# One decode layer on one core: a shorter VectorE program, other load sizes, result stores on exchanged queues, and buffers on lines of 512 bytes

## Chip, cores, metric

One core of a Trainium2 chip. The time is that of the device for one execution, in microseconds (us). The profile's span is shorter than that time: it runs from the first to the last record of the engines, and here that difference (1.24 to 1.55 us on average) turns out to matter. The granted TensorE clock was full (1.00) in most stretches and half (0.50) in some, 0.896 on average in the profile of before.

## The reference, cut to what matters

A decode step for one token: attention over a window of 4096 keys and values, beside a feed-forward block. Everything is bf16.

```python
xn = _layernorm(x)                                # x is [1, 1, 1024]
q  = xn @ wq                                      # wq [1024, 4096], 32 heads of 128
p  = softmax(q @ k[-4096:].T * 128**-0.5)         # 4 groups of keys, 8 heads to each
a  = (p @ v[-4096:]) @ wo                         # wo [4096, 1024]
y  = _layernorm(xn)
b  = gelu(y @ w1 + b1) @ w2 + b2                  # w1 [1024, 3584], w2 [3584, 1024]
out = x + a + b
```

Each weight is used once, so 39.85 MB go through the DMA engines for a single token.

## The kernel before

All loads are issued by SP on one queue in a fixed order: wq, half of K, w1, the other half of K, V, w2, wo. The lists tell how many rows of a weight one load brings. The parts that the change touches, with cuts marked:

```python
WQ_CHUNKS = [1, 3, 2, 2]
W1_CHUNKS = [4, 2, 2]
W2_CHUNKS = [14, 14]
WO_CHUNKS = [13, 9, 4, 2, 2, 1, 1]
...
def moments(ms, T16):                      # mean and variance, called for x and for y
    n = DVE.mark(dve.tensor_reduce(out=ms[:, 0:2], in_=..., axis=AX.X, op=ALU.add))
    dve_dep()
    DVE.mark(dve.tensor_scalar(out=ms[:, 2:4], in0=ms[:, 0:2], scalar1=INV_D, ...))
    ...
DVE.mark(dve.tensor_scalar(out=XNT[:, :], in0=XT16[:, 0:8], ...))     # normalize,
d_xn = DVE.mark(dve.tensor_copy(XNTb[:, :], XNT[:, :]))               # round,
d_xz = DVE.mark(dve.tensor_copy(XZ[:, 96:9 * 97 - 1:97], XNTb[:, :])) # spread
...
for j, nj in enumerate(WO_CHUNKS):         # SP: the loads of wo
    if j0 == FC:
        sp.wait_ge(PE.sem, pe_sc)          # rows 28.. go where K was
    sp.dma_start(wo_at(j0, nj), ...).then_inc(s_wo[j], 16)
...
for j, nj in enumerate(WO_CHUNKS[:-1]):    # PE: two products to a row of wo
    pe.wait_ge(s_wo[j], 16)
    ...
d_out = DVE.mark(dve.tensor_copy(OUT[32:33, :], ACC[1]))
a_out = ACT.mark(act.activation(out=OUT[0:1, :], in_=ACC[0], func=ACTF.Copy))
act.wait_ge(ACT.sem, a_out)
act.dma_start(out_row[:, 0:512], OUT[0:1, :]).then_inc(s_out[0], 16)
sp.wait_ge(DVE.sem, d_out)
sp.dma_start(out_row[:, 512:1024], OUT[32:33, :]).then_inc(s_out[1], 16)
act.wait_ge(s_out[0], 16)
sp.wait_ge(s_out[1], 16)
```

## Time and profile before

| | before |
|---|---|
| time, median of 3 runs | 99.41 us (99.38 to 99.54) |
| span of the profile | 98.1 us |
| bytes on the load queue | 39.85 MB in 24 big loads |
| instructions in VectorE's program | 63 (records of the trace, semaphore waits among them; part 1 of the page counts 57) |

The lines that carry the reading of the stream and of its end are in the prediction below.

```profile
q8 instruction: 1, 0.02, 0.1%
q10 hardware_dynamic: 34, 0.01, 0.1%
q14 instruction: 1, 0.01, 0.0%
```

Two packets within the span do not carry data but instructions: 8192 B on q14 at 77.91 us and 16384 B on q8 at 96.79.

### The profile page before, as it was taken

How to read it: one execution, taken by the hardware profiler on the slowest of the kernel's cores; microseconds unless marked ns; L12 is line 12 of the kernel's file. 1: busy time of each engine (PE TensorE's matmuls, PEld its weight loads, DVE VectorE, ACT ScalarE, POOL GpSimd, SP SyncE). 2: the span in 40 equal slices, each digit the busy share in tenths (PEclk: the TensorE clock that was granted, in tenths of full speed). 3: DMA queues.
4: the chain of work that ended last, by engine and by line, in shares of the span. 5: the costliest groups of instructions: out<-in, count | busy, mean ns of one | idle time of the engine just before them, and what ended most of it. 6: DMA issues, size and time to landing. Idle time of an engine off the chain costs nothing.

```text
span 98.1 us, 1063 instructions
## 1 busy us (share of the span) xinstructions
PE 68.3 (70%) x330; PEld 32.2 (33%) x330; DVE 37.1 (38%) x57; ACT 5.8 (6%) x11; POOL 6.7 (7%) x19
## 2 busy tenths in 40 slices
PE   0002199999992039999999743199991999854991
PEld 0002154555541025666644311033330334211320
DVE  4308562000008999600999544971007000000002
ACT  0500060000002000000000004000000000000002
POOL 6893000000000000000000000000000000000000
PEclk9999999999999555999999999755899579998599
DMA  5999899999998999999999999889989898999950
GB/s 170 447 453 473 379 427 427 427 397 427 449 538 374 386 409 427 456 385 427 427 427 427 427 481 503 374 386 538 386 386 523 361 488 356 436 405 413 412 215 8
DMA packets 3494, 39.89 MB, mean 406 GB/s; under 512 B 402, under 2 KB 420, under 8 KB 932
## 3 DMA queue, kind: packets, MB, share of 16 engines
q1 hardware_dynamic: 3458, 39.85, 95.8%
q8 instruction: 1, 0.02, 0.1%
q10 hardware_dynamic: 34, 0.01, 0.1%
q14 instruction: 1, 0.01, 0.0%
HBM read 39.86 MB, written 0.00 MB: 406 GB/s over the span
## 4 chain that ended last, share of the span: by engine, by line
DMA 81%; DVE 10%; SPq 4%; PE 2%; issue 1%
DMA KV<-in_A_k_cache_dram 43%; DMA KV<-in_A_wo_dram 38%; DVE KV L345 9%; PE PS L406 2%; SPq L176 1%; SPq L160 1%; SPq L166 1%; SPq L427 1%; DVE KV L568 1%; PE PS L558 0%
## 5 line engine op out<-in xcount | busy, mean ns | idle before, releaser
L345 DVE STREAM_TRANSPOSE KV<-KV 128x4096 bf16<-128x4096 bf16 x4 | 17.5, 4424 | 5.8 <-DMA KV<-in_A_k_cache_dram 5.8
L336 PE MATMUL PS<-WA,PT 128*97 x64 | 16.9, 433 | 0.1
L389 PE MATMUL PS<-W,YZ 128*97 x64 | 13.8, 380 | 4.0 <-POOLq L248 4.0
L389 PEld LDWEIGHTS PS<-W,YZ 128*97 x64 | 8.6, 134 | 9.2 <-issue 5.6
L336 PEld LDWEIGHTS PS<-WA,PT 128*97 x64 | 9.1, 142 | 7.6 <-issue 3.0
L549 PE MATMUL PS<-W,OP 128*1 128x512 bf16 x56 | 8.1, 452 | 2.8 <-DMA W<-in_A_wo_dram 2.8
L505 PE MATMUL PS<-KV,PT 128*32 128x512 bf16 x32 | 9.9, 484 | 0.1
L568 DVE CAST KV<-PS 1x512 bf16<-1x512 f32 x1 | 0.7, 683 | 19.9 <-PE PS L558 19.9
L538 PE MATMUL PS<-WA,GT 128*1 128x512 bf16 x56 | 7.9, 451 | 0.0
L406 PE MATMUL PS<-KV,LQ 128*128 x32 | 7.2, 380 | 0.5 <-DVE KV L345 0.5
L286 PE MATMUL PS<-XT,onesf 128*128 128x16 f32 x2 | 0.6, 386 | 8.7 <-DVE XT L282 8.7
L348 DVE STREAM_TRANSPOSE TT<-PS 128x1024 f32<-128x1024 f32 x1 | 1.3, 1251 | 14.1 <-PE PS L336 14.1
L505 PEld LDWEIGHTS PS<-KV,PT 128*32 128x32 bf16 x32 | 3.7, 117 | 5.9 <-issue 4.0
L549 PEld LDWEIGHTS PS<-W,OP 128*1 128x1 bf16 x56 | 2.7, 96 | 8.1 <-issue 3.2
L406 PEld LDWEIGHTS PS<-KV,LQ 128*128 x32 | 3.1, 98 | 4.6 <-issue 1.6
L538 PEld LDWEIGHTS PS<-WA,GT 128*1 128x1 bf16 x56 | 2.7, 96 | 4.7 <-issue 2.5
L510 DVE TENSOR_TENSOR TT<-PS,RM 32x512 f32<-32x512 f32 x1 | 0.7, 679 | 7.2 <-PE PS L505 7.2
L286 PEld LDWEIGHTS PS<-XT,onesf 128*128 128x128 f32 x2 | 0.5, 313 | 8.7 <-DVE XT L282 8.7
L452 ACT ACTIVATE Pe<-PS,NMB 128x512 bf16<-128x512 f32 x2 | 1.3, 684 | 28.3 <-DVE NMB L449 28.3
L570 ACT ACTIVATE KV<-PS 1x512 bf16<-1x512 f32 x1 | 0.6, 587 | 30.7 <-PE PS L558 30.7
L312 PE MATMUL PS<-YT,onesf 128*128 128x16 f32 x2 | 0.6, 384 | 2.4 <-DVE YT L309 2.4
L277 DVE STREAM_TRANSPOSE XTT<-XR 128x256 bf16<-128x256 bf16 x1 | 0.6, 630 | 4.4 <-DMA XR<-in_A_x_dram 4.4
(92 smaller groups left out, 33.7 us busy)
## 6 DMA issues: line engine op xcount, KB each, us to landing
WA<-in_B_w_dram SPq DMA_DIRECT2D x2, 3584.0 KB, 40.5
WA<-in_A_wq_dram SPq DMA_DIRECT2D x2, 2048.0 KB, 18.1
KV<-in_A_k_cache_dram SPq DMA_DIRECT2D x4, 1024.0 KB, 32.9
KV<-in_A_v_cache_dram SPq DMA_DIRECT2D x4, 1024.0 KB, 37.0
W<-in_B_w_dram SPq DMA_DIRECT2D x1, 3584.0 KB, 32.4
W<-in_B_w_dram SPq DMA_DIRECT2D x2, 1792.0 KB, 38.0
W<-in_A_wo_dram SPq DMA_DIRECT2D x1, 3328.0 KB, 34.5
WA<-in_A_wq_dram SPq DMA_DIRECT2D x1, 3072.0 KB, 11.6
```

What stands on the lines that cost most here:

```text
L160: sp.dma_start(WA[:, a:b], wq_pm[:, a:b]).then_inc(s_wq[j], 16)
L286: pe_sum1 = PE.mark(pe.matmul(PS[:, 7 * 512: 7 * 512 + 16], lhsT=onesf[:, :], rhs=XT16[:, 0:16]))
L336: last = pe.matmul(PS[0:97, n * 512:(n + 1) * 512], lhsT=shifted(XZ, s)[:, bass.ds(k, 1), :], rhs=wq_rows[:, bass.ds(k, 1), s * 1024 + n * ...
L345: dve.transpose(out=KT[:, g * W:(g + 1) * W], in_=KT[:, g * W:(g + 1) * W]).then_inc(r_k, 1)
L348: DVE.mark(dve.transpose(out=TT[:, :], in_=PS[:, 0:1024]))
L389: last = pe.matmul(PS[0:97, (2 + n) * 512:(2 + n) * 512 + HW], lhsT=shifted(YZ, s)[:, bass.ds(k, 1), :], rhs=w1_rows[:, bass.ds(k, 1), c: ...
L406: last = pe.matmul(PS[:, (4 + n) * 512:(5 + n) * 512], lhsT=q_blocks[:, bass.ds(g, 1), j, :], rhs=k_blocks[:, bass.ds(g, 1), n, :, j, :], ...
L452: a_exp = ACT.mark(act.activation(out=Pe[:, n * 512:(n + 1) * 512], in_=PS[:, (4 + n) * 512:(5 + n) * 512], func=ACTF.Exp, scale=SCALE, bi ...
L505: last = pe.matmul(PS[0:32, 0:512].rearrange("p (g d) -> p g d", g=HKV), lhsT=PT[:, b * 32:(b + 1) * 32], rhs=Vb[:, b, :, :], start=(b == ...
L538: pe.matmul(ACC[n], lhsT=GT[:, c:c + 1], rhs=W2[:, c * D + n * 512: c * D + (n + 1) * 512], start=False, stop=False)
L549: pe.matmul(ACC[n], lhsT=OP[:, r:r + 1], rhs=wo_at(r, 1)[:, n * 512:(n + 1) * 512], start=False, stop=False)
L568: d_out = DVE.mark(dve.tensor_copy(OUT[32:33, :], ACC[1]))
```

## The change

The intent, as its short description has it: VectorE's program becomes shorter; the two halves of the result go out by each other's queue; the buffers start on lines of 512 bytes; wq comes in 3 loads, w1 in 4, wo in 5.

```diff
-WQ_CHUNKS = [1, 3, 2, 2]
-W1_CHUNKS = [4, 2, 2]
+WQ_CHUNKS = [1, 3, 4]
+W1_CHUNKS = [2, 2, 2, 2]
 W2_CHUNKS = [14, 14]
-WO_CHUNKS = [13, 9, 4, 2, 2, 1, 1]
+WO_CHUNKS = [15, 9, 5, 2, 1]
+WO_IN_W1 = sum(WO_CHUNKS[:2])
 (cut: buffers identb, onesf, XNT, XNTb, YTb go; meanf comes)
+    if nc.sbuf_base % 512:
+        sb("PAD", [128, 512 - nc.sbuf_base % 512], dt.uint8)
     KV = sb("KV", [128, HKV * W + HKV * NBLK * DH], dt.bfloat16)
 (cut: 8 rows of wo instead of 4 go where K was, and the result's buffer OUT moves behind them)
-    DVE.mark(dve.memset(PS[:, 0:4 * 512], 0.0))
+    d_ps = DVE.mark(dve.memset(PS[:, 0:6 * 512], 0.0))
 (cut: POOL makes the masks QMASK and SEL2 that VectorE made; the ones of the sums become 1/D)
-        DVE.mark(dve.tensor_scalar(out=ms[:, 2:4], in0=ms[:, 0:2],
-                                   scalar1=INV_D, scalar2=None, op0=ALU.mult))
-    d_xn = DVE.mark(dve.tensor_copy(XNTb[:, :], XNT[:, :]))
-    d_xz = DVE.mark(dve.tensor_copy(XZ[:, 96:9 * 97 - 1:97], XNTb[:, :]))
+    d_xz = DVE.mark(dve.tensor_scalar(out=XNTb, in0=XT16[:, 0:8], ...))
 (cut: the same for y; waits that follow from these)
-    act.wait_ge(ACT.sem, a_out)
-    act.dma_start(out_row[:, 0:512], OUT[0:1, :]).then_inc(s_out[0], 16)
-    sp.wait_ge(DVE.sem, d_out)
-    sp.dma_start(out_row[:, 512:1024], OUT[32:33, :]).then_inc(s_out[1], 16)
-    act.wait_ge(s_out[0], 16)
-    sp.wait_ge(s_out[1], 16)
+    sp.wait_ge(ACT.sem, a_out)
+    sp.dma_start(out_row[:, 0:512], OUT[0:1, :]).then_inc(s_out[0], 16)
+    act.wait_ge(DVE.sem, d_out)
+    act.dma_start(out_row[:, 512:1024], OUT[32:33, :]).then_inc(s_out[1], 16)
+    sp.wait_ge(s_out[0], 16)
+    act.wait_ge(s_out[1], 16)
```

More of the change, by code (lines that the diff above doesn't have):

```diff
@@ L89, in sb @@
         return nc.alloc_sbuf_tensor(name, shape, dtype)
-    identb = sb("identb", [128, 128], dt.bfloat16)
     identf = sb("identf", [128, 128], dt.float32)
-    onesf = sb("onesf", [128, 128], dt.float32)
+    meanf = sb("meanf", [128, 128], dt.float32)
     SELI = sb("SELI", [128, 32], dt.float32)
@@ L104, in bass_parallel_sum__sliding_block_cached__mixer_channel_mlp__decode_kernel @@
     msx = sb("msx", [128, 8], dt.float32)
-    XNT = sb("XNT", [128, 8], dt.float32)
-    XNTb = sb("XNTb", [128, 8], dt.bfloat16)
     YT16 = sb("YT16", [128, 16], dt.float32)
@@ L109, in bass_parallel_sum__sliding_block_cached__mixer_channel_mlp__decode_kernel @@
     EXPW = sb("EXPW", [128, 1], dt.float32)
-    YTb = sb("YTb", [128, 8], dt.bfloat16)
     TT = sb("TT", [128, 1024], dt.float32)
@@ L125, in bass_parallel_sum__sliding_block_cached__mixer_channel_mlp__decode_kernel @@
     YZ = sb("YZ", [128, 9 * 97 - 1], dt.bfloat16)
+    XNTb = XZ[:, 96:9 * 97 - 1:97]
+    YTb = YZ[:, 96:9 * 97 - 1:97]
     SELB = sb("SELB", [8, 2 * 97], dt.bfloat16)
@@ L133, in bass_parallel_sum__sliding_block_cached__mixer_channel_mlp__decode_kernel @@
     OP = sb("OP", [128, 32], dt.bfloat16)
+    if nc.sbuf_base % 512:
+        sb("PAD", [128, 512 - nc.sbuf_base % 512], dt.uint8)
     KV = sb("KV", [128, HKV * W + HKV * NBLK * DH], dt.bfloat16)
     KT = KV[:, 0:HKV * W]
-    WOX = KV[:, 0:4 * D]
-    OUT = KV[0:33, 4 * D:4 * D + 512]
+    WOX = KV[:, 0:(32 - WO_IN_W1) * D]
+    OUT = KV[0:33, 12 * D:12 * D + 512]
     V = KV[:, HKV * W: HKV * W + HKV * NBLK * DH]
@@ L210, in bass_parallel_sum__sliding_block_cached__mixer_channel_mlp__decode_kernel @@
         base=0, channel_multiplier=1))
-    c_onesf = POOL.mark(pool.memset(onesf[:, :], 1.0))
-    POOL.mark(pool.memset(identb[:, :], 0.0))
+    c_meanf = POOL.mark(pool.memset(meanf[:, :], INV_D))
+    POOL.mark(pool.memset(QMASK[:, :], 1.0))
     pool.wait_ge(POOL.sem, POOL.cnt)
-    c_identb = POOL.mark(pool.affine_select(
-        out=identb[:, :], in_=identb[:, :],
-        pattern=[[-1, 128]], compare_op=ALU.not_equal, fill=1.0,
+    POOL.mark(pool.affine_select(
+        out=QMASK[:, :], in_=QMASK[:, :], pattern=[[-32, 4]], compare_op=ALU.is_ge, fill=0.0,
         base=0, channel_multiplier=1))
+    pool.wait_ge(POOL.sem, POOL.cnt)
+    c_qmask = POOL.mark(pool.affine_select(
+        out=QMASK[:, :], in_=QMASK[:, :], pattern=[[32, 4]], compare_op=ALU.is_ge, fill=0.0,
+        base=31, channel_multiplier=-1))
     POOL.mark(pool.memset(SEL[:, :], 0.0))
@@ L239, in bass_parallel_sum__sliding_block_cached__mixer_channel_mlp__decode_kernel @@
         pattern=[[-16, 2], [-1, 97]], compare_op=ALU.not_equal, fill=1.0, base=0, channel_multiplier=16))
+    POOL.mark(pool.memset(SEL2[:, :], 0.0))
+    for o in (0, 2):
+        pool.wait_ge(POOL.sem, POOL.cnt)
+        c_sel2 = POOL.mark(pool.affine_select(
+            out=SEL2[:, :], in_=SEL2[:, :], pattern=[[-1, 2]], compare_op=ALU.not_equal, fill=1.0,
+            base=-o, channel_multiplier=1))
     POOL.mark(pool.memset(XZ[:, :], 0.0))
@@ L255, in moments @@
         n = DVE.mark(dve.tensor_reduce(
-            out=ms[:, 0:2],
+            out=ms[:, 2:4],
             in_=PS[:, 7 * 512: 7 * 512 + 16].rearrange("p (a k) -> p a k", a=2),
             axis=AX.X, op=ALU.add))
-        dve_dep()
-        DVE.mark(dve.tensor_scalar(out=ms[:, 2:4], in0=ms[:, 0:2],
-                                   scalar1=INV_D, scalar2=None, op0=ALU.mult))
         dve_dep()
@@ L284, in bass_parallel_sum__sliding_block_cached__mixer_channel_mlp__decode_kernel @@
     pe.wait_ge(DVE.sem, d_xsq)
-    pe.wait_ge(POOL.sem, c_onesf)
-    pe_sum1 = PE.mark(pe.matmul(PS[:, 7 * 512: 7 * 512 + 16], lhsT=onesf[:, :], rhs=XT16[:, 0:16]))
+    pe.wait_ge(POOL.sem, c_meanf)
+    pe_sum1 = PE.mark(pe.matmul(PS[:, 7 * 512: 7 * 512 + 16], lhsT=meanf[:, :], rhs=XT16[:, 0:16]))
     dve.wait_ge(POOL.sem, c_identf)
@@ L290, in bass_parallel_sum__sliding_block_cached__mixer_channel_mlp__decode_kernel @@
     dve_dep()
-    DVE.mark(dve.tensor_reduce(out=QMASK[:, :], in_=identf[:, :].rearrange("p (t c) -> p t c", t=4),
-                               axis=AX.X, op=ALU.add))
     DVE.mark(dve.tensor_copy(REPL[:, :].rearrange("p (i c) -> p i c", i=4),
                                       SELI[:, :].unsqueeze(1).to_broadcast([128, 4, 32])))
-    dve.wait_ge(POOL.sem, c_identb)
-    DVE.mark(dve.tensor_tensor(out=SEL2[:, :], in0=identb[0:4, 0:2], in1=identb[0:4, 2:4], op=ALU.add))
     dve.wait_ge(PE.sem, pe_sum1)
     moments(msx, XT16)
-    DVE.mark(dve.tensor_scalar(out=XNT[:, :], in0=XT16[:, 0:8],
-                               scalar1=msx[:, 2:3], scalar2=msx[:, 7:8],
-                               op0=ALU.subtract, op1=ALU.mult))
+    dve.wait_ge(POOL.sem, c_lq)
+    d_xz = DVE.mark(dve.tensor_scalar(out=XNTb, in0=XT16[:, 0:8],
+                                      scalar1=msx[:, 2:3], scalar2=msx[:, 7:8],
+                                      op0=ALU.subtract, op1=ALU.mult))
     dve_dep()
-    d_xn = DVE.mark(dve.tensor_copy(XNTb[:, :], XNT[:, :]))
-    dve_dep()
-    dve.wait_ge(POOL.sem, c_z)
-    d_xz = DVE.mark(dve.tensor_copy(XZ[:, 96:9 * 97 - 1:97], XNTb[:, :]))
-    DVE.mark(dve.tensor_copy(YT16[:, 0:8], XNTb[:, :]))
+    DVE.mark(dve.tensor_copy(YT16[:, 0:8], XNTb))
     dve_dep()
@@ L311, in bass_parallel_sum__sliding_block_cached__mixer_channel_mlp__decode_kernel @@
     pe.wait_ge(DVE.sem, d_ysq)
-    pe_sum2 = PE.mark(pe.matmul(PS[:, 7 * 512: 7 * 512 + 16], lhsT=onesf[:, :], rhs=YT16[:, 0:16]))
+    pe_sum2 = PE.mark(pe.matmul(PS[:, 7 * 512: 7 * 512 + 16], lhsT=meanf[:, :], rhs=YT16[:, 0:16]))
     dve.wait_ge(PE.sem, pe_sum2)
@@ L316, in bass_parallel_sum__sliding_block_cached__mixer_channel_mlp__decode_kernel @@
     ACT.mark(act.activation(out=EXPW[:, 0:1], in_=msy[:, 6:7], func=ACTF.Exp))
-    d_y = DVE.mark(dve.tensor_scalar(
-        out=YTb[:, :], in0=YT16[:, 0:8], scalar1=msy[:, 2:3], scalar2=msy[:, 7:8],
+    d_yz = DVE.mark(dve.tensor_scalar(
+        out=YTb, in0=YT16[:, 0:8], scalar1=msy[:, 2:3], scalar2=msy[:, 7:8],
         op0=ALU.subtract, op1=ALU.mult))
-    dve_dep()
-    d_yz = DVE.mark(dve.tensor_copy(YZ[:, 96:9 * 97 - 1:97], YTb[:, :]))
-    d_zs = DVE.mark(dve.memset(PS[:, 4 * 512:6 * 512], 0.0))
     pe.wait_ge(DVE.sem, d_xz)
@@ L357, in bass_parallel_sum__sliding_block_cached__mixer_channel_mlp__decode_kernel @@
     dve.wait_ge(PE.sem, pe_qx)
-    dve.wait_ge(POOL.sem, c_lq)
     act.wait_ge(PE.sem, pe_qx)
@@ L397, in bass_parallel_sum__sliding_block_cached__mixer_channel_mlp__decode_kernel @@
     pe.wait_ge(ACT.sem, a_lq)
-    pe.wait_ge(DVE.sem, d_zs)
     k_blocks = KT.rearrange("p (g n b j a) -> p g n b j a", g=HKV, n=2, b=16, j=4, a=32)
@@ L420, in wo_at @@
     def wo_at(r, nr):
-        return W1[:, r * D:(r + nr) * D] if r < FC else WOX[:, (r - FC) * D:(r - FC + nr) * D]
+        if r < WO_IN_W1:
+            return W1[:, r * D:(r + nr) * D]
+        return WOX[:, (r - WO_IN_W1) * D:(r - WO_IN_W1 + nr) * D]
     j0 = 0
     for j, nj in enumerate(WO_CHUNKS):
-        if j0 == FC:
+        if j0 == WO_IN_W1:
             sp.wait_ge(PE.sem, pe_sc)
@@ L446, in bass_parallel_sum__sliding_block_cached__mixer_channel_mlp__decode_kernel @@
     pe_nmb = PE.mark(pe.matmul(
-        PS[:, 7 * 512 + 128: 7 * 512 + 129], lhsT=MX4[0:1, :], rhs=onesf[0:1, 0:1]))
+        PS[:, 7 * 512 + 128: 7 * 512 + 129], lhsT=MX4[0:1, :], rhs=identf[0:1, 0:1]))
     dve.wait_ge(PE.sem, pe_nmb)
@@ L483, in bass_parallel_sum__sliding_block_cached__mixer_channel_mlp__decode_kernel @@
     pe.wait_ge(s_b2, 32)
+    pe.wait_ge(POOL.sem, c_sel2)
     pe.wait_ge(DVE.sem, d_nmb)
@@ L493, in bass_parallel_sum__sliding_block_cached__mixer_channel_mlp__decode_kernel @@
     dve_dep()
-    dve.wait_ge(POOL.sem, c_mask)
     DVE.mark(dve.tensor_scalar(out=RM[:, :], in0=MASK[:, :], scalar1=REC[:, 0:1], scalar2=None, op0=ALU.mult))
```

## The prediction

> **What bounds the kernel now.** I read the page first: the slices of the span and the queue table, then the chain that ended last, then the timeline of the end, then the waits, and last the packet records of the trace.
>
> ```profile
> PEclk9999999999999555999999999755899579998599
> DMA  5999899999998999999999999889989898999950
> ...
> q1 hardware_dynamic: 3458, 39.85, 95.8%
> ...
> DMA 81%; DVE 10%; SPq 4%; PE 2%; issue 1%
> ```
>
> The DMA row is at 80% or more from the second slice to the last but one: the 16 DMA engines never pause between about 2 us and 94 us. Counting packets in flight in the trace in steps of 2 us gives 15.95 to 16.4 in every step from 2 to 94 us, so a lull does not hide in the averages. The queue of the big loads (q1) alone is busy 95.8% of the span. The kernel is one long stream of 39.85 MB, and its time is: start of the stream, stream, last landing, and what follows it.
>
> ```profile
> 57.45 0.33 SPq L427
> 57.77 0.04 issue
> 57.82 0.43 SPq L427
> 58.25 0.04 issue
> 58.29 37.43 DMA KV<-in_A_wo_dram
> 95.72 0.04 issue
> 95.76 0.40 PE PS L558 x2
> 96.16 0.02 issue
> 96.19 0.68 DVE KV L568
> ```
>
> These are the last steps of the chain of waits. The chain names a load issued at 58.29 that took 37.43 us; that is queueing behind the stream, not the size of the load (0.25 MB). The steps before it (DVE transposes of K, the PE scores) are in the chain only because they released the issue of that load; 37 us of queue lie between. The true end is: landing 95.72, one row of products 0.40, copy 0.68, then the result's store.
>
> ```profile
> 84.26 2.97 PE L549 MATMUL PS<-W,OP 128*1 128x512 bf16 x26 [0.37 <-DMA W<-in_A_wo_dram]
> 89.61 5.09 PE L549 MATMUL PS<-W,OP 128*1 128x512 bf16 x30 [2.39 <-DMA W<-in_A_wo_dram]
> 94.54 0.95 PE L549 MATMUL PS<-KV,OP 128*1 128x512 bf16 x6
> 95.76 0.38 PE L558 MATMUL PS<-KV,OP 128*1 128x512 bf16 x2 [0.28 <-DMA KV<-in_A_wo_dram]
> ```
>
> That is the timeline of PE (start, duration, instruction, in brackets the idle time before it); the end of all engines' timeline:
>
> ```profile
> 96.18 0.59 ACT L570 ACTIVATE KV<-PS 1x512 bf16<-1x512 f32 x1 [30.67 <-PE PS L558]
> 96.19 0.68 DVE L568 CAST KV<-PS 1x512 bf16<-1x512 f32 x1 [19.89 <-PE PS L558]
> 96.80 0.25 ACTq L572 DMA_DIRECT2D out_dram<-KV  x1
> 96.90 0.32 SPq L574 DMA_DIRECT2D out_dram<-KV  x1
> ```
>
> PE waits for each load of wo, so it follows the stream and does not lead it. Rows of wo land every (89.61 - 84.26)/9 = 0.59 to (95.76 - 94.50)/2 = 0.63 us (94.50 is the first weight load that touches the tile KV); I take 0.61.
>
> [...] median packets take 84 ns at 2048 B, 159 at 4096, 309 at 8192, 535 at 14336 and 1062 at 28672 B. The line through the points at 8192 and 28672 has slope (1062 - 309)/20480 = 0.03677 ns per byte, 27.2 GB/s an engine, 435 GB/s for 16; its intercept is 309 - 301.2 = 7.8 ns, which fits the other sizes within 1 ns. [...] the clock records of this trace change only at multiples of 3.413 us, and windows in which PE was busy 1.52, 0.75, 1.29 and 1.02 us were followed by a half clock, one with 1.81 us was not.
>
> **The change part by part.**
> Alignment: the buffers of the big loads are KV, W1 and WA. In the built programs they start at bytes 38912, 104448 and 161792 of a partition, before and after alike. All are multiples of 512 (76, 204, 316 lines). The small buffers that go away shift the sum, and the 352 bytes of padding put it back. Worth 0.
>
> Loads: wq goes from 4 loads to 3, w1 from 3 to 4, wo from 7 to 5: 24 big loads become 22, with the same bytes. A load puts 8 packets of data and one semaphore packet on each of the 16 engines: 8 x 7.8 + 9 ns (median of the 4-byte packets) = 71 ns. Two fewer: -0.14 us. As the stream is unbroken, that comes off the landing of the last row, whose own size (one row, 0.25 MB) is kept.
>
> VectorE: the prologue loses 8 instructions (5 in the normalizations, two masks, one memset joined to an earlier one). On the chain from x to the first product they save one scaling (start to start 0.20 us: 9.72 to 9.92), a cast and a copy (11.07 to 11.36, 0.29 us) and about 0.12 us of filler ahead of the first sum (its two small masks): 0.20 + 0.29 + 0.12 = 0.6 us before the wq products, which start at 12.49 us. But those products end at 29.36 and release only the issue of w2, which sits 40.5 us in the queue. Nothing on the stream waits: worth 0. The new masks on POOL replace two wide steps; VectorE now waits for POOL's last memset, which ended near 8.1 us, before an instruction at about 10.4. Worth 0.
>
> w1 in four: the first two rows land some 2 x 0.9 MB / 428 GB/s = 4.3 us earlier than the four rows PE waits for at 35.88. PE ends w1 near 47.5 instead of 49.6. The scores after it need the last transpose of K, which VectorE starts when K lands (46.57) and ends at 55.35 either way. Worth 0.
>
> wo in five: the danger. The last three loads are 5, 2 and 1 rows instead of 2, 2, 1, 1, and PE needs 0.216 us a row at full clock and 0.427 at half (512 columns; the weight loads of the half-clock stretch from 90.49 on come 0.43 us apart, a row each, and the 28 rows of w2 took 7.89 us with 3.41 of them at half clock). With the last landing at T, 9 rows are there at T - 4.9 and, at full clock, done at T - 2.9; 5 rows at T - 1.8, done T - 0.75; 2 rows at T - 0.6, done T - 0.2; then the last row on time. At half clock the 9 rows end at T - 1.05 and the rest would run late by up to 1.7 us. [...] Before has the same risk, no smaller: its profile shows the half clock, and still a wait of 0.28 us before the last row.
>
> Result queues: ACT's half is ready at 96.77 and now goes out by SP (0.32 us of issue), VectorE's at 96.87 by ACT (0.25). Before: the later issue began at 96.90 and took 0.32, ending at 97.22, and 0.9 us later the kernel ended at 98.1. After: 96.80 + 0.32 = 97.12 and 96.90 + 0.25 = 97.15. The later one ends 0.07 us sooner: -0.07.
>
> Sum: -0.14 - 0.07 + 0.03 = -0.18; 99.41 becomes 99.2 us.
>
> **The rivals.**
> First: PE becomes the end. For it: the half clock at 90.0 to 93.4 in this very profile, and a load of 5 rows third from last. Against it: full-clock slack of 0.4 us or more at each load. If it holds in all runs: 100.0 to 101.
> Second: the prologue matters after all, so that its 0.6 us comes off as well: 98.6. For it: the chain of waits passes DVE for 10%. Against it: that share is K's transposes, and the queue is full behind them.
> Third: larger alignment or packet effects, if the engines' slowest one (its last data packet ended at 95.38 when most ended by 94.6) catches up: down to 98.5. Nothing in the change is aimed at one engine.
> Fourth: a later issue, as 8 rows instead of 4 of wo now wait for the scores at 57.4. The stream has over 18 us of earlier loads queued then (w2's second half lands about 76), so nothing.
>
> **Range and chances.** The three runs of before spread 0.16 us; the sum above is uncertain by about 0.2 on each side. Range 98.9 to 99.5. Faster by over 2% means under 97.42, which needs 2 us that the stream doesn't have: its bytes alone are 39.85 MB / 435 GB/s = 91.6 us, against some 93.5 used. Slower by over 2% means 101.4, the first rival at its worst.
>
> **What would show it.** Right: q1's packets fall by 2 x (128 of data + 16 of semaphores) = 288, from 3458 to near 3170, its DMA row stays full, the last wo row lands 0.1 to 0.2 us earlier, PE waits for DMA before the last row, and SP's result issue comes first. Wrong: PE busy without a gap over the last 5 us and the last product well after the landing (first rival), or a hole in the DMA row, or a last landing earlier by 0.5 us or more, which would mean that the stream's start or its rate had moved.

The sum came to -0.18 us, so 99.2: -0.14 for two loads fewer and -0.07 for the result queues, both worked out from the trace of before, and +0.03 for wo in five. The working of the +0.03 is cut, so that term stands as the author's estimate alone: it took the windows of the clock for a rule, which no run shows.

## The result

| | before | changed |
|---|---|---|
| median | 99.39 us (99.24 to 99.54, 4 runs) | 99.0 us (98.83 to 99.1, 4 runs) |
| span of the profile | 98.1 us | 97.7 us |
| packets of the load queue | 3458 | 3170 |
| VectorE's program | 63 instructions | 53 |

The ratio is 0.9959, with a 95% interval of 0.9938 to 0.9979. The time fell by 0.4 us where 0.2 was predicted: within the range, but twice the sum. The page of the changed kernel, its DMA row and queue table:

```profile
DMA  5999999999999999999999999999999999899960
...
q1 hardware_dynamic: 3170, 39.85, 96.1%
q8 instruction: 1, 0.02, 0.1%
q10 hardware_dynamic: 34, 0.01, 0.1%
```

The stream is as full as before, with the 288 packets fewer that were foretold. The line q14 is gone: no packet of instructions moves while the stream runs (the one of q8 starts at 96.12 us). Now the last 0.7 us in which load packets are in flight, 94.8 to 95.5 us, first in before (each column is a fortieth of that stretch):

```profile
DMA  3003030033000030000300030000300000000000
...
q1 hardware_dynamic: 11, 0.02, 6.9%
```

and the same stretch of the changed kernel:

```profile
DMA  0000000000000000000000000000000000000000
```

In before a handful of packets, one after the other, are still under way when 14 of the 16 engines have nothing left: one DMA engine is late, a second less so, and the last landing (95.72) waits for it. The changed kernel has none. The end of its PE timeline (start, duration, instruction, idle time before it):

```profile
84.78 3.40 PE L548 MATMUL PS<-W,OP 128*1 128x512 bf16 x30 [0.24 <-DMA W<-in_A_wo_dram]
90.18 3.57 PE L548 MATMUL PS<-W,OP 128*1 128x512 bf16 x18 [2.00 <-DMA W<-in_A_wo_dram]
93.54 1.95 PE L548 MATMUL PS<-KV,OP 128*1 128x512 bf16 x14
95.32 0.38 PE L557 MATMUL PS<-KV,OP 128*1 128x512 bf16 x2
```

Unlike before there is no wait left in front of the last two groups: in this execution PE ended late, not the stream. And the end of all engines:

```profile
95.74 0.59 ACT L569 ACTIVATE KV<-PS 1x512 bf16<-1x512 f32 x1 [29.58 <-PE PS L557]
95.74 0.68 DVE L567 CAST KV<-PS 1x512 bf16<-1x512 f32 x1 [18.80 <-PE PS L557]
96.35 0.32 SPq L571 DMA_DIRECT2D out_dram<-KV  x1
96.46 0.25 ACTq L573 DMA_DIRECT2D out_dram<-KV  x1
```

SP issues first now, and the later issue ends 0.25 us after its start instead of 0.32, as foretold.

**One DMA engine followed through.** Every one of the 16 engines carries the same sequence of packets, eight to a big load, back to back. The trace has the start and the duration of each packet, so the sequences can be put together: the next packet of an engine is the one of the next size that starts 3 to 4 ns before the last ended. In before, 14 of the 16 sequences end between 94.31 and 94.64 us, one at 95.03 and one at 95.38. The one that ends last has a hole of 303 ns that ends at 78.22 us, and the packet of instructions on q14 is at 77.91 to 78.22, 309 ns long. Its next packet of data then took 1518 ns where its equals took 987: 531 more, by far the longest excess in the stream. Together 0.83 us on one engine, which is about how far it ended behind the median engine (95.38 against 94.53). VectorE did not wait for these instructions: it had ended its last work before a long wait at 76.29.

**Two theories for the experiments.** The fetch: with 63 instructions VectorE's program is what brings the q14 packet of 8192 B at 77.91 us; it takes 309 ns on one of the 16 engines that the stream fills, that engine ends last (95.38), and its last row of wo is what the kernel waits for. Rival: engines scatter by chance, and what gained is the smaller number of loads.

### The profile page after: what moved, and what is told of

It reads as the page before. It is cut to its first block, busy times and chain, and to the rows that moved or that the text cites. A ratio compares the mean times of both kernels' runs of the same rounds, so it can differ in the third digit from the quotient of the medians.

```text
span 97.7 us, 1056 instructions
## 1 busy us (share of the span) xinstructions
PE 68.9 (71%) x330; PEld 32.0 (33%) x330; DVE 36.6 (37%) x49; ACT 5.8 (6%) x11; POOL 7.1 (7%) x23
## 3 DMA queue, kind: packets, MB, share of 16 engines
q1 hardware_dynamic: 3170, 39.85, 96.1%
## 4 chain that ended last, share of the span: by engine, by line
DMA 84%; PE 9%; SPq 4%; issue 1%; DVE 1%; POOLq 0%
DMA W<-in_A_wo_dram 43%; DMA W<-in_B_w_dram 41%; PE PS L548 5%; PE PS L387 3%; SPq L178 1%; SPq L168 1%; SPq L162 1%; DVE KV L567 1%; SPq L426 0%; PE PS L557 0%; POOLq L260 0%
## 5 line engine op out<-in xcount | busy, mean ns | idle before, releaser
L335 PE MATMUL PS<-WA,PT 128*97 x64 | 15.8, 410 | 1.4 <-POOLq L260 1.2
L387 PE MATMUL PS<-W,YZ 128*97 x64 | 14.7, 387 | 1.2 <-POOLq L260 1.2
L335 PEld LDWEIGHTS PS<-WA,PT 128*97 x64 | 8.6, 134 | 8.2 <-issue 4.1
L403 PE MATMUL PS<-KV,LQ 128*128 x32 | 7.8, 399 | 2.3 <-DVE KV L344 2.3
L548 PE MATMUL PS<-W,OP 128*1 128x512 bf16 x48 | 7.0, 451 | 2.2 <-DMA W<-in_A_wo_dram 2.2
L295 PE MATMUL PS<-XT,meanf 128*128 128x16 f32 x2 | 0.6, 386 | 9.1 <-DVE XT L291 9.1
L548 PEld LDWEIGHTS PS<-W,OP 128*1 128x1 bf16 x48 | 2.2, 92 | 6.6 <-DMA W<-in_A_wo_dram 2.5
L295 PEld LDWEIGHTS PS<-XT,meanf 128*128 128x128 f32 x2 | 0.5, 312 | 9.1 <-DVE XT L291 9.1
L205 DVE MEMSET PS<- 128x3072 f32 x1 | 2.6, 2618 | 0.6 <-issue 0.6
L430 DVE TENSOR_REDUCE MXP<-PS 128x1 f32<-128x1024 f32 x1 | 1.2, 1225 | 2.7 <-PE PS L403 2.7
```

Of the source, the lines that this page charges most:

```text
L205: d_ps = DVE.mark(dve.memset(PS[:, 0:6 * 512], 0.0))
L335: last = pe.matmul(PS[0:97, n * 512:(n + 1) * 512], lhsT=shifted(XZ, s)[:, bass.ds(k, 1), :], rhs=wq_rows[:, bass.ds(k, 1), s * 1024 + n * ...
L387: last = pe.matmul(PS[0:97, (2 + n) * 512:(2 + n) * 512 + HW], lhsT=shifted(YZ, s)[:, bass.ds(k, 1), :], rhs=w1_rows[:, bass.ds(k, 1), c: ...
L403: last = pe.matmul(PS[:, (4 + n) * 512:(5 + n) * 512], lhsT=q_blocks[:, bass.ds(g, 1), j, :], rhs=k_blocks[:, bass.ds(g, 1), n, :, j, :], ...
L430: d_mxp = DVE.mark(dve.tensor_reduce(out=MXP[:, 0:1], in_=PS[:, 4 * 512:6 * 512], axis=AX.X, op=ALU.max))
L548: pe.matmul(ACC[n], lhsT=OP[:, r:r + 1], rhs=wo_at(r, 1)[:, n * 512:(n + 1) * 512], start=False, stop=False)
```

## The experiments

The first four ran on one chip and share 11 runs of before (median 99.29), the next four on another (11 runs, 99.44), the last four share 9 runs of before (99.38). All results were correct.

| run | median, us | ratio to before | 95% interval | time less span |
|---|---|---|---|---|
| e1 changed kernel | 98.87 | 0.9960 | 0.9948 to 0.9972 | 1.38 |
| e2 VectorE longer by 10 | 99.60 | 1.0034 | 1.0017 to 1.0051 | 1.43 |
| e3 loads of before | 99.00 | 0.9965 | 0.9952 to 0.9978 | 1.42 |
| e4 result queues of before | 98.66 | 0.9944 | 0.9925 to 0.9963 | 1.24 |
| e5 changed kernel | 98.98 | 0.9957 | 0.9930 to 0.9984 | 1.41 |
| e6 as e4 | 98.72 | 0.9922 | 0.9910 to 0.9935 | 1.26 |
| e7 no padding | 99.39 | 0.9996 | 0.9983 to 1.0009 | 1.40 |
| e8 18 loads | 98.86 | 0.9937 | 0.9924 to 0.9949 | 1.44 |
| e9 PE kept busy | 100.02 | 1.0062 | 1.0048 to 1.0077 | 1.47 |
| e10 18 loads, queues of before | 98.67 | 0.9928 | 0.9914 to 0.9942 | 1.32 |
| e11 e9 and e10 | 99.83 | 1.0042 | 1.0027 to 1.0057 | 1.29 |
| e12 VectorE longer by 5 | 99.03 | 0.9968 | 0.9953 to 0.9984 | 1.55 |

Time less span is the mean over a kernel's executions, each of which has both (spans to 0.1 us). For before it is 1.28, 1.27 and 1.28 in the three calls.

### The yardstick

> The changed kernel as it is, again, as the yardstick of the runs of this call. Both theories: 98.85 to 99.1 us, and no instruction packet on the DMA engines while the stream runs.

98.87 us, and no q14 line.

> The changed kernel a third time, as the yardstick of this call: 98.8 to 99.05 us.

98.98 us, with a spread of 98.71 to 99.66. Single executions of this kernel differ by more than the effects at hand.

### The fetch of instructions

> The changed kernel with ten tiny memsets added to VectorE's program while it waits for x (53 instructions become 63, as many as before). Theory of the fetch: the profile of before has one instruction packet of 8192 B, 309 ns, at 77.9 us on one DMA engine, and that engine ended last; it comes back here, and the time rises by 0.2 to 0.35 us over the changed kernel, to 99.2 to 99.35. Rival (the engine that ended last in before was chance): the time stays at 98.9 to 99.1, packet or no packet.

```diff
     d_xr0 = DVE.mark(dve.memset(XR[:, :], 0.0))
+    for i in range(10):
+        dve.memset(FILL[:, i:i + 1], 0.0)
```

99.60 us, 0.73 above e1: more than was expected, and slower than before by 0.3%. Two stretches of its trace, 77.0 to 77.6 us and 94.8 to 95.5:

```profile
q14 instruction: 1, 0.01, 3.2%
```

```profile
DMA  0003000030000300030000000000000000000000
...
q1 hardware_dynamic: 5, 0.01, 3.1%
```

The packet of instructions is back (3.2% of 16 engines in 0.6 us is 0.31 us), and so is the single late engine. The data packet of 30720 B that began at 77.43, as the fetch ended, took 1668 ns against 1138 of its equals: 530 ns more, the same as in before. The last engine ended at 95.19, the median one at 94.37. The rival, by which the time should not move, is out. That the added memsets by themselves cost it is made unlikely by the next run, in which half of them cost nothing.

That the packet belongs to VectorE's program shows in its time too. VectorE's last instruction before its long wait, in before and then in e2:

```profile
76.10 0.19 DVE L529 CAST OP<-PS 128x32 bf16<-128x32 f32 x1 [0.35 <-PE PS L524]
```

```profile
75.32 0.19 DVE L531 CAST OP<-PS 128x32 bf16<-128x32 f32 x1 [0.38 <-PE PS L526]
```

The fetch starts 1.62 us after the end of this instruction in both (77.91 and 77.13).

> The changed kernel with five tiny memsets in VectorE's program (58 instructions): a look at where between 53 and 63 the fetch comes in. Either a packet of 8192 B on queue 14 within the stream and 99.3 to 99.7 us, or none and 98.8 to 99.1. Both theories of the fetch's place allow either; only a fetch packet without the longer time, or the longer time without it, would speak against the fetch as the cause.

The same edit with `range(5)`: 58 instructions, 99.03 us, no q14 packet, all engines done by 94.74. So the step lies above 58 and at or below 63 instructions, and it is a step: five more instructions leave the ratio at 0.9968 beside 0.9957 to 0.9960 of the yardsticks, and ten bring it to 1.0034. No run shows why e2 pays more (0.73) than what before gets back (0.46, below); its single executions lie between 99.37 and 99.87.

> The changed kernel with the 24 loads of before (wq 1 3 2 2, w1 4 2 2, wo 13 9 4 2 2 1 1). Theory of the fetch: two loads more cost 0.14 us of stream, PE is no longer late at the end (worth up to 0.15), so 0.0 to +0.15 over the changed kernel, 99.0 to 99.15. Rival (the loads are the whole gain): +0.3 to +0.4, 99.3 to 99.4.

```diff
-WQ_CHUNKS = [1, 3, 4]
-W1_CHUNKS = [2, 2, 2, 2]
+WQ_CHUNKS = [1, 3, 2, 2]
+W1_CHUNKS = [4, 2, 2]
-WO_CHUNKS = [15, 9, 5, 2, 1]
-WO_IN_W1 = sum(WO_CHUNKS[:2])
+WO_CHUNKS = [13, 9, 4, 2, 2, 1, 1]
+WO_IN_W1 = sum(WO_CHUNKS[:4])
```

99.00 us: 0.13 above e1, 0.29 below before. The loads are not the gain. This kernel has the loads of before and no fetch, and it keeps PE's wait of 0.25 us ahead of the last row, although its clock was half from 90.05 to 93.47:

```profile
95.27 0.38 PE L557 MATMUL PS<-KV,OP 128*1 128x512 bf16 x2 [0.25 <-DMA KV<-in_A_wo_dram]
```

Its mean span is 97.56 us, that of before in the same rounds 98.02: the shorter program is worth 0.46 us within the span (the exchanged result queues, in which the two differ too, change nothing there, as shown below).

### PE's clock at the end, and the same fetch on another engine

> The changed kernel with six products into an unused bank after the first load of wo[...]. Theory: in part of the executions of the changed kernel (its profile, e8's) the half clock makes the last row start 0.2 us later than its landing allows; without it 0.05 to 0.15 us come off on average, ratio to before 0.9945 to 0.995 instead of 0.996, and the last products start 0.33 to 0.39 us after the last data packet in the profile. Rival (the clock doesn't matter at the end): ratio 0.996 as for the changed kernel.

The six products were meant to fill the 2.00 us that PE waits before 90.18 in the changed kernel's profile. That its clock would then stay full was the guess, and the profiles do not make it a rule: in the changed kernel's the clock was half after a stretch (87.25 to 90.66) with PE busy 1.41 us, in e1's it was full after the same stretch with 1.44.

```diff
             r += 1
+        if j == 0:
+            for _ in range(6):
+                pe.matmul(PS[64:65, 4 * 512:5 * 512], lhsT=GT[:, 0:1], rhs=W2[:, 0:512], start=True, stop=True)
```

A miss: 100.02 us, by the ratios about 1.0 us slower than the changed kernel, where 0.1 was to be won. Three answers say why: the queue table of the page, that of the stretch 80 to 82 us, and the last line of PE's timeline:

```profile
q8 instruction: 2, 0.03, 0.1%
```

```profile
q8 instruction: 1, 0.02, 2.9%
```

```profile
96.42 0.38 PE L560 MATMUL PS<-KV,OP 128*1 128x512 bf16 x2
```

All the other kernels have one q8 packet, after the stream (96.07 to 97.05 us in e1). With twelve instructions more on PE there is a second one, of 16384 B, within the stream. One engine has a hole of 905 ns up to 81.70 and then a data packet 506 ns longer than its equals; it ended at 96.03, the median engine at 94.36, and the last products could start only at 96.42 (95.04 in e1). So the fetch theory holds for another engine's program too, with a packet twice as large and a hole three times as long. The six products ran only from 90.23 us on, as the late engine held up the first load of wo too (PE waited for it until 86.21, in e1 until 84.72), so whether the half clock matters at the end is not answered by this run.

What is left on that question is a comparison of profiles. In the changed kernel's own profile the clock was granted at half from 90.66 to 94.07:

```profile
90.66:94.07 3.41, 3.41 (x20) 1.04 (x18) 0.00 (x0) 0.00 (x0) 0.00 (x0) 0.50 0.99 410
```

and in e1's at full (columns: stretch and length; busy PE, PEld, DVE, ACT, POOL; clock; DMA share; GB/s):

```profile
90.66:94.07 3.41, 2.41 (x25) 0.79 (x20) 0.00 (x0) 0.00 (x0) 0.00 (x0) 1.00 0.97 404
```

The last products began 0.57 us after the last load packet in the first, 0.34 in the second. The same 0.56 to 0.57 is in e8 and e10, which also had the half clock there, and 0.33 to 0.36 in e4, e5, e6 and e12, which had it not. So the half clock goes with about 0.2 us, in three of eight profiles, all with the last wo loads of 5, 2 and 1 rows; before and e3, with 2, 2, 1 and 1, had the half clock at about the same time and still waited for the last row. It was not tested by a run that changes the clock alone: that stays argued, not shown.

### The result queues

> The changed kernel with the result queues as before (ACT's half by ACT, VectorE's half by SP). Both theories: +0.07 us from the issue times, 99.0 to 99.15; the later issue is SP's, 0.32 us long. Rival: 0, the two halves' stores end together.

```diff
-    sp.wait_ge(ACT.sem, a_out)
-    sp.dma_start(out_row[:, 0:512], OUT[0:1, :]).then_inc(s_out[0], 16)
-    act.wait_ge(DVE.sem, d_out)
-    act.dma_start(out_row[:, 512:1024], OUT[32:33, :]).then_inc(s_out[1], 16)
+    act.wait_ge(ACT.sem, a_out)
+    act.dma_start(out_row[:, 0:512], OUT[0:1, :]).then_inc(s_out[0], 16)
+    sp.wait_ge(DVE.sem, d_out)
+    sp.dma_start(out_row[:, 512:1024], OUT[32:33, :]).then_inc(s_out[1], 16)
```

(and the two waits at the end likewise). 98.66 us, 0.21 below e1 where 0.07 above was expected. The end of e4:

```profile
94.91 0.38 PE L557 MATMUL PS<-KV,OP 128*1 128x512 bf16 x2
...
95.95 0.25 ACTq L571 DMA_DIRECT2D out_dram<-KV  x1
96.05 0.32 SPq L573 DMA_DIRECT2D out_dram<-KV  x1
```

and of e1:

```profile
95.04 0.38 PE L557 MATMUL PS<-KV,OP 128*1 128x512 bf16 x2
...
96.07 0.32 SPq L571 DMA_DIRECT2D out_dram<-KV  x1
96.17 0.25 ACTq L573 DMA_DIRECT2D out_dram<-KV  x1
```

From the last products to the end of the later issue: 1.46 us in e4 and 1.38 in e1, so the 0.07 is there. But by the packet records of both, the store's packet starts 0.43 to 0.44 us after SP's issue ends and 0.49 to 0.51 after ACT's, and the last packet of the store ends 1.94 us after the last products in both, as it does in before. Within the span the swap is worth nothing.

> The result queues as before, repeated, since e4 came out 0.2 us faster than the changed kernel where its profile shows the last store ending 1.94 us after the last products began, as in the changed kernel and in before (the swap is worth 0 there). Theory: the swap is worth 0 and e4 was a lucky series; within 0.1 of e5. Rival: the swap costs 0.2, and this is again 0.2 below e5; then the last landing must again be earlier, from the start of the stream on.

Again 0.26 below e5, on another chip: not a lucky series. My theory that the swap is worth 0 fell, and so did the rival's reason (an earlier landing): the mean span is 97.44 against 97.65 in the noisy e5, and 97.48 against 97.52 in e4 and e1. The steady difference is in the last column of the table. Where SP waits for the later store (before, e4, e6, e10, e11), the time exceeds the span by 1.24 to 1.32 us on average; where ACT does (the other eight series), by 1.38 to 1.55. So some 0.14 us of the swap's cost lie outside the span. What happens there no trace shows. That it goes with the swap, the means of all the series show without exception; but single executions overlap (before 1.20 to 1.38, e1 and e5 1.35 to 1.49), and e12 with 1.55 lies as far from e1 as the swap moves it. The swap exchanges the queue of the later store and the engine that waits for it at once, so no run says which of the two counts.

### The padding

> The changed kernel without the padding: KV, W1 and WA start 160 bytes past a line of 512 instead of on it. Theory [...]: 8192-byte packets stay at 309 ns and the time within 0.1 of e5. [...]

```diff
-    if nc.sbuf_base % 512:
-        sb("PAD", [128, 512 - nc.sbuf_base % 512], dt.uint8)
```

99.39 us, 0.41 above e5: without the padding the changed kernel is as slow as before. The padding itself gains nothing over before, whose buffers lay on lines of 512 without it; it prevents a loss as large as the whole gain. The theory is out. The rival, packets longer and a longer time, is right in kind; the loss is smaller than it put it. The big buffers start 160 bytes past a line. From V on, the packets are longer by a little: 18432 B took 689 ns instead of 686, 28672 B 1066 instead of 1062, 30720 B 1142 instead of 1138. The packets of wq and w1 and those of K did not (309, 535, 912 and 1213 ns as before), which no run explains. An engine carries 88 data packets from V on; their mean excess, size by size, adds up to 0.32 us. The median engine ended at 94.78, 0.32 later than the mean of 94.46 of the six profiles with 22 loads and no fetch, so within the stream this accounts for the loss. From the last load packet to the last products it took 0.47 us instead of 0.33 to 0.39; that part is from one profile and unexplained.

### Fewer loads

> The changed kernel with 18 big loads instead of 22 (wq 4 4, w1 4 4, w2 28; wo as it is). If a load costs 8 x 7.8 + 9 = 71 ns of stream, -0.28 us against e5, 98.5 to 98.7; q1 shows 3170 - 576 = 2594 packets. Rival (a load's cost hides behind the pipelined packets): 0. Other rival: PE starts later in wq, w1 and w2 and the end is late: +0.2 or more.

```diff
-WQ_CHUNKS = [1, 3, 4]
-W1_CHUNKS = [2, 2, 2, 2]
-W2_CHUNKS = [14, 14]
+WQ_CHUNKS = [4, 4]
+W1_CHUNKS = [4, 4]
+W2_CHUNKS = [28]
```

98.86 us, 0.12 below e5, with 2594 packets. The estimate of 0.28 is too large. The median engine's end is the cleaner measure: 94.53 and 94.55 us with 24 loads (before, e3), 94.36 to 94.59, mean 94.46, with 22 (the six profiles of them on the lines of 512 and without a fetch), 94.25 to 94.31 with 18 (e8, e10, e11). That is 0.04 us a load, not 0.071. The packet records say why. An engine's next packet starts 3 to 4 ns before the last one ends, so the 309 ns of a packet of 8192 B are not what it costs the stream: from start to start it is 305.9 ns, and 1058.8 for 28672 B. The line through all sizes from V on, 2048 to 28672 B, has the slope of the prediction (435 GB/s) and an intercept of 4.7 ns, not 7.8; a semaphore packet takes 6 ns from start to start, not 9. 8 x 4.7 + 6 = 44 ns a load. In the profile of e8 PE was also late by 0.2.

> 18 big loads and the result queues as before. If both effects stand and add: -0.15 (queues, outside the span: time minus span 1.25 instead of 1.4 us) and -0.1 to -0.28 (loads) against the changed kernel, ratio to before 0.991 to 0.993. Rival (e4 and e6 were lucky): 0.9935 to 0.995, as e8.

Both edits: 98.67 us, ratio 0.9928, in the range expected, but no better than e4 or e6 (0.9944, 0.9922), which have the queues alone.

> All three together: 18 big loads, result queues as before, six products[...]. Theory: the loads' 0.28 us now shows whole, ratio to before 0.990 to 0.992, no execution with a late last row. Rival: as e10.

99.83 us, a miss for the same reason as e9: a q8 packet in the stream with a hole of 905 ns, one engine ending at 95.85 when the median ended at 94.30.

**A version that beats both kernels**: the changed one with the result queues of before (e4 and e6), 0.6% and 0.8% under before and 0.21 and 0.26 us under the changed kernel in the same rounds.

## Why the prediction was right or wrong, point by point

- **The bound**: right. The stream stays full in every kernel (the row shows a 4 in one slice of e8 and e10, but it counts a packet, of up to 2.1 us there, in the slice where it starts; the records have 16 in flight throughout), and each gain or loss is in when the last landing comes or in what follows it. (One reading is off: the row is at 80% or more up to the third slice from the end; the last but one is 5.)
- **Alignment, worth 0**: right for the change, as the buffers lay on lines of 512 before and after. But it was a part that could lose everything: leaving it out costs 0.4 us (e7).
- **Loads, -0.14**: right in kind, too large. The profiles with 24 and with 22 loads differ by 0.08 us at the median engine. The term mis-sized is the cost of a packet: the prediction took the intercept of the durations, 7.8 ns, where the packets of an engine overlap and the intercept from start to start is 4.7 ns, so 0.044 us a load and 0.09 for two. Its own count of packets in flight, up to 16.4 on 16 engines (16.6 in the last step, 92 to 94 us), was the hint.
- **VectorE, worth 0**: this is the step that failed. The prologue's shorter chain is indeed worth nothing; the wq products began at 12.23 instead of 12.49 and nothing came of it. (0.26 us, not 0.6: POOL, with the new masks, ended its last memset at 8.79 instead of 8.12, and VectorE's copy XT<-XTT took 0.77 us instead of 0.17 and ended with it, so that the first sum began 0.33 us later. No run isolates this.) But the number of instructions itself was worth 0.46 us, because it removed the fetch. The prediction even named the late engine (its third rival: last packet at 95.38 when most ended by 94.6) and dismissed it with "Nothing in the change is aimed at one engine". The line for q14 in the page of before and the words "shorter VectorE program" were the pointers to it.
- **wo in five, PE late, +0.03**: the mechanism is seen in three profiles of eight at 0.2 us each, 0.08 on average. No run isolates it. The "full-clock slack of 0.4 us or more at each load" of the first rival contradicts the prediction's own sums, which leave 0.15 us after the 5 rows and 0.2 after the 2; in e1 PE waited 0.17 and 0.16 us there. The clock windows that it lists are no rule: they leave out one at half clock with 2.60 us of work, after which the clock stayed half, and one from 8.09 us with 0.61, after which it stayed full; and a window with 1.66 us of work in the changed kernel's profile (29.22 to 32.63) was followed by a half clock.
- **Result queues, -0.07**: wrong in sign. The shorter issue (0.25 us against 0.32) is there, the store of ACT's queue starts later by as much (0.49 to 0.51 us after the issue against 0.43 to 0.44), and outside the span the swap costs about 0.14 us.
- **Sum**: -0.46 (fetch) - 0.08 (loads) + 0.14 (queues) = -0.40, and 99.39 to 99.0 was measured; PE's lateness, not isolated, is left out. That 99.0 lay inside the predicted 98.9 to 99.5 is luck: the missed gain of 0.46 and the missed loss at the queues (0.14, and the 0.07 that did not come) partly cancel.
- **What would show it wrong**: "a last landing earlier by 0.5 us or more" was written as the sign that the stream had moved. The last load packet of the changed kernel ended at 94.75 instead of 95.38, 0.63 earlier; that test did its work. The first rival's sign came too, in part: in the changed kernel's profile PE has no gap after 90.18, and its last products begin 0.57 us after the last load packet.

## What to carry to other kernels

In a kernel that keeps the DMA engines full to the end, look for packets of instructions within the stream: here one such packet put one engine of 16 behind by 0.83 us, the last landing waited for that engine, and 8192 B, 0.02% of the bytes, cost 0.46 us, 0.5% of the time. Before adding instructions to an engine's program (even idle-time ones), check whether the profile's queue table gains an instruction packet, and before calling a saving of instructions hidden, check whether it loses one. And compare the timed runs with the span: what differs outside the span, here with which engine issues and awaits the later store, no view of the span shows.
